# Two attentions in one program: when the second one starts, and what GpSimd does beside VectorE's trees

## The chip, the cores and the metric

One core of a Trainium2 chip. The metric is the device time of one execution in microseconds (us). A kernel is run several times and the median is given; one further execution is taken by the hardware profiler, and all readings of the trace are of that one. The span is the time from the first to the last instruction of the program on the core.

## The reference

Two multi-head layers over 2048 tokens of width 512, with 32 heads of 16, each with its own input and weights. A is softmax attention; B is linear attention with a feature map of two softmaxes. The result is both outputs side by side.

```
def A(x, wqkv, wo):
    q, k, v = heads(x @ wqkv)                          # 32 heads, 2048 x 16 each
    p = softmax(q @ k.T * 16 ** -0.5)                  # 2048 x 2048 for each head
    return concat_heads(p @ v) @ wo

def B(x, wqkv, w_phi, wo):
    q, k, v = heads(x @ wqkv)
    pq, pk = q @ w_phi, k @ w_phi                      # 16 x 16 for each head
    phi_q = [softmax(pq), softmax(-pq)]                # 32 features
    phi_k = [softmax(pk), softmax(-pk)]
    kv, z = phi_k.T @ v, phi_k.sum(tokens)
    return concat_heads((phi_q @ kv) / (phi_q @ z + 1e-6)) @ wo

out = concatenate([A, B], axis=-1)                     # 2048 x 1024, bfloat16
```

## The kernel before, in words

The program is written by a planner. A Python loop at the end of the function walks through numbered steps and appends instructions to one list for each engine (`_Plan`); each operation names what it depends on, and the plan turns that into semaphore waits. The loop chooses what TensorE does next by a small model of the engines' clocks (`_Clock`): the numbers in it decide only the order of the instructions. On the chip each engine takes its list strictly in order, and an instruction that waits holds up all that stands behind it on its engine. SyncE's list holds nearly all DMAs, in order as well.

**Attention A.** Heads are taken four at a time (a group g, rows 32r of the PE array for the four), queries 512 at a time (c): 8 x 4 = 32 units. A unit is cut into segments of 128-query tiles (`SPLIT`: mostly 2 and 2, the first unit 1, 1, 2, the last 2, 1, 1). Each of the 1024 steps (`order`) takes one query tile, one chunk of 512 keys (kc) and one pair of heads:

- `emit_m1` (L974): two matmuls put the scores of 128 queries x 512 keys for two heads into two PSUM banks; four banks are used by turns.
- `emit_r1` (L988): VectorE takes the maximum over the keys, 128 x 1024 values in one reduction.
- When a segment's steps are done, `emit_mchain` joins the maxima of the key chunks (L998, VectorE), GpSimd splits the negated maximum into two bfloat16 parts (L1004 to L1007), SyncE transposes them (L1009) and writes them as extra rows into QT (L1011). With them the scores come out with the maximum subtracted.
- From `LAGX` = 8 steps after the segment's end on, `block_go` computes the scores again, transposed, 512 columns in a block (L1041), ScalarE takes the exponential (L1048) into one of `RING` = 15 buffers, and `pv_go` multiplies with V (L1094). A column of ones in V gives the sum. There are 2048 blocks.
- After a unit, `emit_xev` copies the sums and products out (X, L458), `emit_rec` takes the reciprocals (a power on GpSimd, L1214) and spreads them by DMA (L1216, L1219), and `emit_mul` divides (L1229, GpSimd). `oproj_job` and, for the last 512 queries, `acc_job` and `emit_last` apply the output matrix (L1298 writes the last of it).

Where TensorE would have little to do, the planner puts in matmuls of zeros (L1178, L1193), which change nothing in the result.

**The head.** x comes in four chunks of 512 tokens by transposing DMAs on SyncE (L302). The weights for K and Q of the first groups come on ScalarE's queue, V's weights (columns 1024 to 1536) on SyncE's queue behind the third chunk of x (`load_w`, L296). `proj` computes K, Q and V (L498, L485); a chunk of keys can be scored only when its K exists. The table `XA` tells the planner from which time on it may order work on a chunk of x. The steps of the first segment need a new chunk of keys every two steps; two steps of the second segment are put in behind the first two.

**Attention B** fills gaps. 32 feature maps (`fm`, 16 for K, then 16 for Q) are planned from step `FM0` on, one every `FMSTEP` steps. Of a map: four matmuls and a copy by ScalarE (pB); two maps together go through `red`, a tree of eight small maxima and minima on VectorE (L660, L663, L665); then on GpSimd the subtraction (`sub`, L680, L682), on ScalarE the exponential (`ex`, L688), on GpSimd `sums` (L695 to L706), for K maps `rec` (a power, L718), and `mul` (L738). Four K maps at a time are multiplied with V (`kv_job`, added up by L794, masked by L798). A Q map goes on through a transposing DMA (`q_t`, L815), a matmul (`y_job`, L823), a copy to yB by ScalarE, `q_rc` (L841, L843 and a power, L846) and `q_mul` (L853) on GpSimd, a second transposing DMA (L862) into oTB, the output matmul (`ob_job`, L870), a copy to outB by ScalarE and the DMA to the output (L877). One Q map's `y_job` may only be planned when the `q_mul` of the map before it is. `pool_slot` hands out GpSimd's time in steps, so that planned work doesn't meet; `later(step, f)` runs f when the planner comes to a step; `add_job` queues matmuls for a gap from a step on, due at `by`.

Of the kernel before, what the change touches and what calls it, by code (L numbers as in the profile page):

```python
# [49 lines left out]
class _Plan:  # L50

    def __init__(self):
        self.streams = {}

    def add_stream(self, key, sem, step=1):
        self.streams[key] = _Stream(key, sem, step)

    def op(self, key, fn, deps=(), signal=True):
        s = self.streams[key]
        need = s.merge(deps)  # L60
        if not signal:
            s.items.append((fn, need, None))
            return None
        s.seq += 1
        clock = dict(s.known)
        clock[key] = s.seq
        s.items.append((fn, need, key))
        return _Tok(key, s.seq, clock)
# [80 lines left out]
def bass_concat_heads__softmax_full_mha__linear_kernel_hedgehog__prompt_kernel(  # L149
# [12 lines left out]
    SPLIT = {**{u: (2, 2) for u in range(NU)}, 0: (1, 1, 2), NU - 1: (2, 1, 1)}  # L162
    RING = 15
    BATCH = 4
    PIECE = 1
# [11 lines left out]
    TOP = 12.0  # L177
    FM0 = 172
    FMSTEP = 26
    units = [(g, c) for c in range(NQC) for g in range(NG)]  # L180
# [10 lines left out]
    for v, (u, q0, nq) in enumerate(segs):  # L191
        steps = [(v, pr, qt, kc) for kc in range(NKC) for qt in range(q0, q0 + nq) for pr in range(2)]
        if u == 0 and v == 1:
            order[2:2] = steps[0:2]
            steps = steps[2:]
        order += steps
# [9 lines left out]
    with contextlib.ExitStack() as es:  # L206
# [87 lines left out]

        def load_w(queue, lo, hi):
            t_wa[lo] = P.dma(queue, dsem("wa%d" % lo), lambda e: e.dma_start(wA[:, :, lo:hi], wa_v[:, :, lo:hi]))  # L296

# [3 lines left out]
        for c in range(NQC):  # L301
            t_xa[c] = P.dma("sp", dsem("xa%d" % c), lambda e, c=c: e.dma_start_transpose(  # L302
                xAT[:, :, c * 512:(c + 1) * 512], A_x[0][c * 512:(c + 1) * 512, :]))
            if c == 2:
                load_w("sp", 1024, 1536)
        load_w("sp", 128, 512)
# [51 lines left out]
        def later(slot, fn):  # L358
            calls.setdefault(slot, []).append(fn)

        pool_busy = [(q - 1, q + 2) for q in seg_end]

# [17 lines left out]

        ck = _Clock(8.5)
        ring_free = [(0.0, 4), (0.0, 5), (0.0, 6)]
# [153 lines left out]

        XA = (6.0, 11.0, 14.5, 18.5)
        need = [(4, "k", 0, 1), (6, "k", 0, 2), (8, "k", 0, 3)]
        need += [(LAG + 2 + kt, "v", kt, 0) for kt in range(NKT)]
        need += [(32 + 8 * c, "k", 1, c) for c in range(NKC)] + [(31, "q", 1, 0)]  # L540
        for at, t in enumerate(sorted(need)):
            c = t[2] // 4 if t[1] == "v" else t[3]
            add_job(at, *proj(*t[1:]), by=t[0] - 4, when=lambda c=c: ck.pe > XA[c])
        at = 30
        for g in range(2, NG, 2):
            for t in group(g):
                add_job(at, *proj(*t), by=at + 10)
                at += 6
        at = 200
        for c in range(1, NQC):  # L550
# [7 lines left out]
        for b, kind in ((4, "k"), (5, "q")):  # L558
# [3 lines left out]
            bank_reader[b] = fin(b, tok, 0)  # L562
        ck.act = 9.0

# [59 lines left out]
        for i in range(8):  # L624
            add_job(146 + 3 * i, *fold_job(1 - i // 4, i % 4), by=150 + 3 * i)

        kv_last = {}

        def fm(n):
# [8 lines left out]
            def p_fin(b, tok, tau):  # L638
                cx["p"] = aevac(pB[:, i, :], PS[:, b, :], [tok] + use(("p", i)))
                later(tau + 2, lambda: red(tau + 2))  # L640
                return cx["p"]
# [11 lines left out]
            def red(tau):  # L653
# [8 lines left out]
                for w in (4, 2):  # L662
# [5 lines left out]
                    [ts[k]] + use(("m", 0)) + use(("m", 1))) for k in range(2)]  # L668
                ck.extra += 1.85
                for c in (cx, first_map[0]):  # L670
                    c["mx"] = c["mn"] = ts[1]
                s = pool_slot(tau + 3, 2)
                later(s, lambda fn=first_map[1]: fn(s))
# [54 lines left out]
            def mul(tau):  # L728
# [15 lines left out]
                if x == 1:  # L744
                    kst[st] = cx
                    if st % 4 == 3:
                        for hf in range(2):
                            add_job(tau + 4, *kv_job(st // 4, hf))
                else:
                    later(tau + 4, lambda: q_t(st, cx, tau + 4))  # L750
# [61 lines left out]
        def q_t(st, cx, tau):  # L812
            i = st % 2
            k = st % 4
            cx["pt"] = P.dma("sp", d_pt[i], lambda e: e.dma_start_transpose(phiT[:, i], phiB[k]),  # L815
                             [cx["phi"], last_proj["q"]] + use(("pt", i)))
            users[("phi", k)] = [cx["pt"]]
            for hf in range(2):
                add_job(tau + 10, *y_job(st, cx, hf), when=lambda: st == 0 or st - 1 in q_done)

# [30 lines left out]
        def q_mul(st, cx, tau):  # L851
# [9 lines left out]
            def tr():  # L861
                cx["ot"] = P.dma("sp", d_ot[i], lambda e: e.dma_start_transpose(oTB[:, i], oB),  # L862
                                 [t] + use(("ot", i)))
                users[("o", 0)] = [cx["ot"]]
                add_job(tau + 14, *ob_job(st, cx))
            later(tau + 3, tr)
# [14 lines left out]

        first_map = []
        for n in range(2 * NKT):
            fm(n)
# [137 lines left out]
        def block_go(tau):  # L1022
# [11 lines left out]
            ck.run_tiled(r, start)  # L1034
            ck.heat.append((start, 0.25))
            g, c = units[u]
            slot = B % RING
# [37 lines left out]
        def pv_go(tau):  # L1075
# [15 lines left out]
            for j in range(per):  # L1091
                for B in Bs:
# [7 lines left out]
                    deps = []  # L1100
            ck.run_full("col", start, ck.ROW + 0.01)
            ck.heat.append((start, 1.0))
# [333 lines left out]
```

## Time and profile before

| | us |
|---|---|
| median of 3 runs | 1305.03 (1292.47 to 1312.32) |
| the profiled execution | 1295.11 |
| its span | 1293.4 |
| PE busy | 1222.3 (95%) |
| VectorE (DVE) busy | 1213.8 (94%) |
| ScalarE (ACT) busy | 1165.0 (90%) |
| GpSimd (POOL) busy | 632.8 (49%) |
| mean granted TensorE clock | 0.984 |

How to read it: busy time is the union of an engine's instructions; waits on semaphores and the issuing of DMAs are not counted. Reductions of VectorE overlap a little at their ends, so that their mean of 1215 ns is longer than the distance from one to the next. A row of a timeline gives the start, the time to the end of the last of the merged instructions, the engine, the line, what is written and read, and in brackets the idle time of the engine ahead of it and who ended it. SPq is SyncE's queue: its time is that of issuing, not of the transfer. The granted clock is the share of TensorE's full clock that the throttle let through.

### The profile page before, as it was taken

The numbers are of one execution on the slowest core, as the hardware profiler recorded it, in microseconds if no ns is written. First come the engines' busy times: TensorE is split into PE (matmuls) and PEld (weight loads), VectorE is DVE, ScalarE is ACT, GpSimd is POOL, SyncE is SP. The second block draws the span as 40 slices with busy tenths as digits, with TensorE's granted clock in tenths as the row PEclk, the third lists the DMA queues.
The fourth block names the chain that finished last, engine by engine and source line by source line (L and its number), as shares of the span: only waits on it lengthen the run. The fifth ranks groups of instructions, "written<-read, shape, count | busy, mean of one in ns | idle before, by whom it ended". The sixth has DMA issues, their size and how long they took to land.

```text
span 1293.4 us, 38893 instructions
## 1 busy us (share of the span) xinstructions
PE 1222.3 (95%) x16990; PEld 487.5 (38%) x16990; DVE 1213.8 (94%) x1229; ACT 1165.0 (90%) x2296; POOL 632.8 (49%) x724
## 2 busy tenths in 40 slices
PE   7999999999999999999999999999999999999998
PEld 2433333333333333334333333333333333333346
DVE  6999999999999899999999999999999999999930
ACT  3899999998988899999999989999989999999993
POOL 3311020255556465566574654565555466556562
PEclk9999999999999799999999989999989999999999
DMA  6134200001011001101101002121211121123121
GB/s 132 37 60 78 41 9 9 8 8 13 9 15 20 7 11 11 12 8 13 12 9 17 15 8 25 17 32 17 33 12 30 27 33 18 31 23 29 13 34 40
DMA packets 84259, 31.55 MB, mean 24 GB/s; under 512 B 71864, under 2 KB 82104, under 8 KB 84088
## 3 DMA queue, kind: packets, MB, share of 16 engines
q1 hardware_dynamic: 82744, 28.54, 15.8%
q8 instruction: 133, 2.18, 0.7%
q10 hardware_dynamic: 1344, 0.52, 0.2%
q14 instruction: 38, 0.31, 0.1%
HBM read 3.16 MB, written 4.19 MB: 6 GB/s over the span
## 4 chain that ended last, share of the span: by engine, by line
ACT 51%; PE 29%; DVE 18%; issue 1%; DMA 1%; SPq 1%; POOL 0%; DVEq 0%; ACTq 0%
ACT pT L1048 45%; DVE part L988 16%; PE PS L1041 6%; PE PS L974 4%; PE PS L1193 4%; PE PS L1094 3%; PE PS L1178 2%; PE PS L498 2%; PE PS L643 2%; ACT eB L688 1%; PE PS L485 1%; PE PS L870 1%; PE PS L898 1%; ACT X L458 1%; ACT pB L458 1%
## 5 line engine op out<-in xcount | busy, mean ns | idle before, releaser
L988 DVE TENSOR_REDUCE part<-PS 128x2 f32<-128x1024 f32 x1024 | 1174.8, 1215 | 21.6 <-PE PS L974 9.9
L1048 ACT ACTIVATE pT<-PS 128x512 bf16<-128x512 f32 x2048 | 1055.2, 636 | 75.4 <-PE PS L1041 38.1
L1041 PE MATMUL PS<-QT,KT 32*128 32x256 bf16 (+1 forms) x4224 | 666.1, 272 | 19.6 <-ACT pT L1048 2.1
L1178 PE MATMUL PS<-zmv,ones_t 32*128 32x512 bf16 x1755 | 595.9, 387 | 0.6 <-ACT X L458 0.4
L974 PE MATMUL PS<-KT,QT 32*128 32x512 bf16 x2048 | 452.1, 388 | 17.3 <-DVE part L988 11.8
L1041 PEld LDWEIGHTS PS<-QT,KT 32*128 32x128 bf16 x4224 | 226.5, 92 | 369.7 <-ACT pT L1048 222.9
L1004 POOL TENSOR_SCALAR stage<-mrow 128x8 bf16<-128x8 f32 (+1 forms) x66 | 15.8, 239 | 466.6 <-DVE mrow L998 466.6
L1094 PE MATMUL PS<-pT,VP 128*17 128x256 bf16 (+1 forms) x4224 | 205.5, 275 | 14.0 <-ACT pT L1048 4.8
L1193 PE MATMUL PS<-zmv,ones_t 128*17 128x256 bf16 x3640 | 169.0, 279 | 2.5 <-ACT X L458 2.0
L974 PEld LDWEIGHTS PS<-KT,QT 32*128 32x128 bf16 x2048 | 118.4, 91 | 110.3 <-DVE part L988 74.8
L1178 PEld LDWEIGHTS PS<-zmv,ones_t 32*128 32x128 bf16 x1755 | 144.2, 91 | 3.0 <-PE PS L1178 1.2
L1094 PEld LDWEIGHTS PS<-pT,VP 128*17 128x17 bf16 x4224 | 62.3, 88 | 125.1 <-ACT pT L1048 60.2
L1193 PEld LDWEIGHTS PS<-zmv,ones_t 128*17 128x17 bf16 x3640 | 73.5, 90 | 88.6 <-issue 77.7
L1214 POOL TENSOR_TENSOR lr<-lr,neg 128x16 f32<-128x16 f32 x31 | 90.6, 2922 | 16.9 <-DMA lr<-X 16.9
L846 POOL TENSOR_TENSOR den_t<-den_t,neg 128x32 f32<-128x32 f32 x16 | 87.5, 5467 | 1.3
L718 POOL TENSOR_TENSOR wB<-wB,neg 128x32 f32<-128x32 f32 x16 | 87.0, 5440 | 0.1
L1229 POOL TENSOR_TENSOR QT<-X,Yd 128x256 bf16<-128x256 f32 x62 | 44.0, 731 | 66.8 <-DMA Yd<-Yd 66.8
L738 POOL TENSOR_TENSOR wA<-eB,rB 128x512 bf16<-128x512 bf16 x64 | 66.9, 1069 | 0.6
L680 POOL TENSOR_TENSOR uB<-pB,mB 128x512 f32<-128x512 bf16 x32 | 33.5, 1047 | 27.4 <-DVE mB L665 27.4
L695 POOL TENSOR_TENSOR sB<-eB 128x512 f32<-128x512 bf16 x32 | 36.9, 1153 | 11.8 <-ACT eB L688 11.8
L643 PE MATMUL PS<-WKp,xBT 128*128 128x512 bf16 x128 | 38.0, 389 | 1.8 <-ACT pT L1048 0.2
L698 POOL TENSOR_TENSOR sB<-sB 128x256 f32<-128x256 f32 x64 | 36.1, 564 | 5.0
(90 smaller groups left out, 586.2 us busy)
## 6 DMA issues: line engine op xcount, KB each, us to landing
Yd<-Yd SPq DMA_DIRECT2D x124, 32.0 KB, 3.2
out_dram<-xAT SPq DMA_DIRECT2D x16, 128.0 KB, 1.9
KT<-oct_t SPq DMA_DIRECT2D x24, 64.0 KB, 2.1
QT<-oct_t SPq DMA_DIRECT2D x24, 64.0 KB, 2.0
out_dram<-OA SPq DMA_DIRECT2D x12, 128.0 KB, 1.8
mcols<-stage SPq DMA_TRANSPOSE x66, 2.2
QT<-mcols SPq DMA_DIRECT2D x62, 4.0 KB
wA<-in_A_wqkv_dram SPq DMA_DIRECT2D x2, 384.0 KB, 4.9
```

The costliest lines, as they stand in the source:

```text
L643: add_job(slot, mm_pieces(lambda e, b, ct: e.matmul(PS[:, b, :], xBT[:, ct, st * 128:(st + 1) * 128], Wf[:, x, ct, :], start=(ct == 0), st ...
L718: t = P.op("pool", lambda e: e.tensor_tensor(wB[:, n % 4, :], wB[:, n % 4, :], neg1[:, 0:1].broadcast_to([128, 32]), ALU.pow), [cx["r"], t ...
L738: t = P.op("pool", lambda e, a=a: e.tensor_tensor(f4[:, :, a, :], e4[:, :, a, :], r2[:, :, 1 - a].unsqueeze(2).broadcast_to([128, H, 16]), ...
L846: cx["rd"] = P.op("pool", lambda e: e.tensor_tensor(den_t[:, :], den_t[:, :], neg1[:, 0:1].broadcast_to([128, 32]), ALU.pow), [t, t_neg])
L974: tok = P.op("pe", lambda e, r=r, bank=2 * (q1 % 2) + i: e.matmul(PS[:, bank, :], QT[32 * r:32 * r + 32, g, q0:q0 + 128], KT[32 * r:32 * r ...
L988: r1[q1] = P.op("dve", lambda e: e.tensor_reduce(part[:, u % 2, 2 * pr:2 * pr + 2, qt, kc], PS[:, b:b + 2, :], AX.X, ALU.max), deps)
L1041: m2_t[B] = P.op("pe", lambda e, j=j: e.matmul(PS[:, bank, j * w:j * w + w], KT[32 * r:32 * r + 32, g, (kt + j) * 128:(kt + j + 1) * 128], ...
L1048: exp_t[B] = P.op("act", lambda e: e.activation(pT[:, slot, :], PS[:, bank, :], ACT.Exp, scale=0.25), [m2_t[B], slot_reader.get(slot)])
L1094: tok = P.op("pe", lambda e, B=B, r=r, j=j: e.matmul(PVB[32 * r:32 * r + 17, lo:lo + w], VP[:, kt + j, 4 * g + r, :], pT[:, B % RING, j * ...
L1178: fill_tok[0] = P.op("pe", lambda e: e.matmul(PS[:, 7, :], ones_t[32 * r:32 * r + 32, :], zmv[32 * r:32 * r + 32, :], start=False, stop=Fa ...
L1193: P.op("pe", lambda e, cq=cq: e.matmul(PS[32 * cq:32 * cq + 17, bank, 0:256], ones_t[:, 0:17], zmv[:, 0:256], start=(bank != 7), stop=(ban ...
L1214: rec = P.op("pool", lambda e: e.tensor_tensor(lr[:, ub, :], lr[:, ub, :], neg1[:, 0:1].broadcast_to([128, 16]), ALU.pow), [lr_t[u], t_neg])
```

## The change

- B's feature maps are planned from step 152 instead of 172 (`FM0`), one every 25 steps instead of 26 (`FMSTEP`); the folding of B's weights (`fold_job`) and A's later Q projections are planned 20 to 30 steps sooner. `y_job` is planned 8 instead of 10 steps behind the first transpose, `ob_job` 9 instead of 14 behind `q_mul`. `kv_job` may only be planned when the V parts of its four maps are.
- `_Plan.fence`: behind each tree, the first operation that the plan appends to GpSimd's list also waits for the tree's last operation. `red` is put in a slot in which GpSimd has nothing planned; the slots reserved at a segment's end are shortened by one step at the front.
- V's weights are loaded on ScalarE's queue when the first chunk of x has landed, no longer on SyncE's.
- Six steps of the second segment stand among those of the first instead of two: two behind each of its first three pairs (`EARLY`). The first segment ends at step 14 instead of 10, so the first exponentials are planned from step 22 instead of 18.
- Constants of the planner's clock model change: its start, `XA`, and a small charge for blocks that are made of several matmuls.

The built programs hold the same number of operations on VectorE (1229) and GpSimd (720); one DMA moves from SyncE's list to ScalarE's, and TensorE's list has 16274 matmuls instead of 16990, the difference being matmuls of zeros.

```
@@ class _Plan
+        self.fence = []
...
     def op(self, key, fn, deps=(), signal=True):
         s = self.streams[key]
+        if key == "pool" and self.fence:
+            deps = list(deps) + self.fence
+            del self.fence[:]
         need = s.merge(deps)
...
+    EARLY = 3
-    FM0 = 172
-    FMSTEP = 26
+    FM0 = 152
+    FMSTEP = 25
...
         if u == 0 and v == 1:
-            order[2:2] = steps[0:2]
-            steps = steps[2:]
+            for k in range(EARLY):
+                order[2 + 4 * k:2 + 4 * k] = steps[2 * k:2 * k + 2]
+            steps = steps[2 * EARLY:]
...
-        def load_w(queue, lo, hi):
-            t_wa[lo] = P.dma(queue, dsem("wa%d" % lo), lambda e: e.dma_start(wA[:, :, lo:hi], wa_v[:, :, lo:hi]))
+        def load_w(queue, lo, hi, deps=()):
+            t_wa[lo] = P.dma(queue, dsem("wa%d" % lo), lambda e: e.dma_start(wA[:, :, lo:hi], wa_v[:, :, lo:hi]), deps)
...
-            if c == 2:
-                load_w("sp", 1024, 1536)
+            if c == 0:
+                load_w("act", 1024, 1536, [t_xa[0]])
...
-        pool_busy = [(q - 1, q + 2) for q in seg_end]
+        pool_busy = [(q, q + 2) for q in seg_end]
...
-        ck = _Clock(8.5)
+        ck = _Clock(9.6)
...
-        XA = (6.0, 11.0, 14.5, 18.5)
+        XA = (6.0, 11.2, 14.0, 18.6)
...
-            add_job(at, *proj(*t[1:]), by=t[0] - 4, when=lambda c=c: ck.pe > XA[c])
+            add_job(at, *proj(*t[1:]), by=t[0] - 4, when=lambda c=c, v=t[1] == "v": ck.pe > max(XA[c], 11.8 * v))
...
-        at = 200
+        at = 170
...
-        ck.act = 9.0
+        ck.act = 9.6
...
-            add_job(146 + 3 * i, *fold_job(1 - i // 4, i % 4), by=150 + 3 * i)
+            add_job(125 + 3 * i, *fold_job(1 - i // 4, i % 4), by=130 + 3 * i)
...
@@ def p_fin
-                later(tau + 2, lambda: red(tau + 2))
+                s = tau + 2 if i == 0 else pool_slot(tau + 2, 3) + 1
+                later(s, lambda: red(s))
@@ def red
+                fence.append(ts[1])
...
-                s = pool_slot(tau + 3, 2)
+                s = pool_slot(tau + 2, 2)
@@ def mul
-                            add_job(tau + 4, *kv_job(st // 4, hf))
+                            add_job(tau + 4, *kv_job(st // 4, hf), when=lambda: all(
+                                "v" in kst.get(4 * (st // 4) + j, ()) for j in range(4)))
@@ def q_t
-                add_job(tau + 10, *y_job(st, cx, hf), when=lambda: st == 0 or st - 1 in q_done)
+                add_job(tau + 8, *y_job(st, cx, hf), when=lambda: st == 0 or st - 1 in q_done)
@@ def q_mul
-                add_job(tau + 14, *ob_job(st, cx))
+                add_job(tau + 9, *ob_job(st, cx))
...
+        P.fence = fence = []
...
@@ def block_go
+            start += 0.012 * (per - 1)
+            ck.rows[r] += 0.012 * (per - 1)
@@ def pv_go
-            ck.run_full("col", start, ck.ROW + 0.01)
+            ck.run_full("col", start, ck.ROW + 0.01 + 0.008 * (per - 1))
```

## The prediction, made before the changed kernel ran

> **What bounds the kernel now.** I read the busy shares and the costliest groups first, then the timelines of the two ends of the span, and last the stretches in which the granted clock fell.
>
> ```profile
> DVE  6999999999999899999999999999999999999930
> ACT  3899999998988899999999989999989999999993
> ...
> PEclk9999999999999799999999989999989999999999
> ...
> L988 DVE TENSOR_REDUCE part<-PS 128x2 f32<-128x1024 f32 x1024 | 1174.8, 1215 | 21.6 <-PE PS L974 9.9
> ```
>
> VectorE's 1024 maximum reductions (one a step, emit_r1) set the pace: they follow each other every 1.13 us, 1024 x 1.13 = 1157 us of a span of 1293.4 us. The first starts at 10.19 us, the last ends at 1239.6 us, so a step takes 1.20 us in the mean; then 53.8 us follow without reductions. The time above 1157 us lies in four places: that end, the head, the trees and the clock.
>
> The end, timeline of ScalarE and then of SyncE from 1240 us on:
>
> ```profile
> 1268.11 0.60 ACT L458 ACTIVATE xAT<-PS 128x512 bf16<-128x512 f32 x1 [1.13 <-PE PS L870]
> ...
> 1277.64 0.60 ACT L458 ACTIVATE xAT<-PS 128x512 bf16<-128x512 f32 x1 [5.12 <-PE PS L870]
> 1289.22 0.60 ACT L458 ACTIVATE xAT<-PS 128x512 bf16<-128x512 f32 x1 [10.98 <-PE PS L870]
> ```
>
> ```profile
> 1271.19 1.69 SPq L1298 DMA_DIRECT2D out_dram<-eB x2
> ...
> 1278.65 1.19 SPq L862 DMA_TRANSPOSE xAT<-WQp  x1
> 1289.84 0.34 SPq L877 DMA_DIRECT2D out_dram<-xAT  x1
> ```
>
> A's last output (L1298) is issued at 1272.54 and lands some 3.2 us later (fastest landing of that line), at 1275.7. All behind it is B: two more results through L862 and L870, with ScalarE idle 5.12 and 10.98 us between them. B's last output (L877) lands 1.7 us after 1289.84, at 1291.5.
>
> A tree (the pairwise maxima and minima of L660 to L665) by itself and beside GpSimd, VectorE's timeline, then GpSimd's:
>
> ```profile
> 245.44 0.75 DVE L660 TENSOR_TENSOR uB<-pB 128x512 bf16<-128x512 bf16 x2
> ...
> 247.24 3.52 DVE L988 TENSOR_REDUCE part<-PS 128x2 f32<-128x1024 f32 x3
> ```
>
> ```profile
> 370.03 1.73 DVE L660 TENSOR_TENSOR uB<-pB 128x512 bf16<-128x512 bf16 x2
> ...
> 372.82 2.34 DVE L988 TENSOR_REDUCE part<-PS 128x2 f32<-128x1024 f32 x2
> ```
>
> ```profile
> 369.88 1.60 POOL L1229 TENSOR_TENSOR QT<-X,Yd 128x256 bf16<-128x256 f32 x2
> ```
>
> Alone, a tree holds up the reductions for 247.24 - 245.44 = 1.80 us; beside two products of L1229 for 2.79 us. The same reading gives 3.28 us at 429.81 (beside L738 and L1214), 2.89 at 501.05 (L1229) and 2.84 at 747.84 (L794, L798): 0.99 + 1.48 + 1.09 + 1.04 = 4.6 us for four of the sixteen trees.
>
> The stretches in which TensorE had half its clock, as a table (span, then busy time of PE, PEld, DVE, ACT, POOL, granted clock):
>
> ```profile
> 433.00:454.50 21.50, 20.19 (x198) 6.16 (x197) 16.16 (x16) 15.49 (x29) 8.24 (x10) 0.52 0.12 8
> 754.80:765.10 10.30, 10.30 (x111) 3.50 (x110) 7.77 (x9) 7.72 (x15) 5.08 (x9) 0.50 0.02 5
> 846.90:850.50 3.60, 3.50 (x47) 1.08 (x46) 2.41 (x3) 2.92 (x7) 2.58 (x1) 0.53 0.02 5
> 963.00:970.00 7.00, 7.00 (x65) 2.08 (x66) 4.41 (x4) 4.51 (x8) 2.42 (x5) 0.51 0.46 38
> ```
>
> In them VectorE idles 5.34 + 2.53 + 1.19 + 2.59 = 11.7 us. The first two begin 4 and 7 us after the crowded trees at 429.81 and 747.84; the fourth follows a wait of ScalarE for GpSimd's L853 (2.9 us at 959.8).
>
> The head, VectorE's timeline:
>
> ```profile
> 10.19 3.49 DVE L988 TENSOR_REDUCE part<-PS 128x2 f32<-128x1024 f32 x3 [0.49 <-PE PS L974]
> 14.56 1.23 DVE L988 TENSOR_REDUCE part<-PS 128x2 f32<-128x1024 f32 x1 [0.89 <-PE PS L974]
> 16.27 2.36 DVE L988 TENSOR_REDUCE part<-PS 128x2 f32<-128x1024 f32 x2 [0.48 <-PE PS L974]
> 19.28 2.36 DVE L988 TENSOR_REDUCE part<-PS 128x2 f32<-128x1024 f32 x2 [0.65 <-PE PS L974]
> 23.15 3.49 DVE L988 TENSOR_REDUCE part<-PS 128x2 f32<-128x1024 f32 x3 [1.51 <-PE PS L974]
> ```
>
> Behind the first start, four waits of 0.89 + 0.48 + 0.65 + 1.51 = 3.5 us for the next chunk of K.
>
> **The change part by part**, against the profiled execution, 1295.1 us (span 1293.4).
>
> B sooner and closer (FM0, FMSTEP). The last map's planned step goes from 172 + 31 x 26 = 978 to 152 + 31 x 25 = 927: 51 steps, 51 x 1.20 = 61 us. B's last output then lands near 1230 us, well before A's. The chain from last map to last output keeps its length, some 105 us (evictions of pB at 1186 us, landing at 1291.5); even 30 us more would stay covered. The span now ends with A: 1275.7 against 1291.5 is -15.8 us. Of B's work inside A's own last 36 us, ScalarE loses four L458 evictions of yB (1.5 us), two of outB (1.2 us) and 1.1 us of waiting for L870: 3.8 us at most, nothing if 45 exponentials wait for something else; I take -2.5. The same work now lies in the middle, beside reductions. There ScalarE was busy 930 of the 1000 us from 200 to 1200; a map costs it 0.60 + 1.08 + about 0.6 us, 2.3 us, and at 25 steps instead of 26 this is 0.3% of its time more. I take 0, at most +3 (0.3% of 1000 us, if all of it became backlog).
>
> Trees on an idle GpSimd (Plan.fence, and red now asks for a free slot). At most -4.6, at least 0; ten of the sixteen fences fall on L680, which needed the tree anyway, so they add nothing; the other six hold an L1229, an L794, a power or the start of q_rc for at most one tree, 1.8 us. Queued behind them is B's work, with slack since B is off the end, and once a maximum split (L1004), whose blocks are due eight steps (9.6 us) later and whose row was sent off 3.2 us (median) to 7.4 us after the maximum here. I take -4. A sentence of the Trainium skill, "SBUF — State Buffer", "SBUF: two separate sides", calls VectorE's and GpSimd's shared port an exclusive lock held for the whole instruction. By it a tree that meets a power would wait for all of its 2.9 or 5.5 us, and as four fences have a power right ahead of them in GpSimd's queue, up to 4 x 2.9 = 11.6 us would be given back, 1276. This trace agrees for products, not for powers: the tree at 820.55 ran beside the 5.55 us of L846 and took 1.95 us.
>
> Clock. If the crowded trees opened the two stretches behind them, 5.34 + 2.53 = 7.9 us go with them. The bounds are -11.7 (no fall at all) and 0 (others fall instead). I take -5.
>
> Head (EARLY = 3, V's weights). Six steps of the second part now stand between the chunks of K, two behind each pair, so each chunk has 4 x 1.13 = 4.5 us instead of 2.3; K's second chunk also stands ahead of the first V projection, which waited at 12.73 us for V's weights. At most -3.5, at least 0; I take -3, as the chunks' projections took about 3 us from pair to pair in the rows above. V's weights (512 KB) leave SyncE's queue: the fourth transpose of x and all behind it are issued 0.6 us sooner. On ScalarE's queue they wait for x's first chunk (6.45 us); nothing stands behind them there before the first eviction at 13.8 us. The first part now ends at step 14 instead of 10 and the exponentials begin four steps later in number, 4.5 us, of which 3 us are made up: +1 at worst, taken as 0. A sentence of the Trainium skill, "Trainium Kernel Development and Optimization", "Key Constraints", speaks against this part: queues share the same 16 DMA engines, so a second one saves issue time alone. The engines' share is 0.70 from 10 to 26 us, at 142 GB/s; by it 512 KB among x's chunks could take 3.6 us from them and the head's term would be 0, 1268.
>
> Waits of B on transposes (y_job 2 steps sooner, ob_job 5 steps or 6 us sooner). In the last stage above, L862's result lands 4.1 us (its slowest) after 1278.65 and L870 starts at 1288.15: 5.4 us later. With 6 us less TensorE would stop 0.6 us; the other stages have more, so 0. kv_job's new condition holds a job until its V exists: 0.
>
> Sum: -15.8 - 2.5 - 4 - 5 - 3 = -30.3, 1264.8 us. The profiled execution is 9.9 us under the median of the runs shown (1305.03; 1292.47 to 1312.32). Nothing in VectorE's durations can make such a spread (1202 to 1229 ns each), so I put it to the clock stretches, which the change thins out, and add nothing to the value but 10 us to the upper bound.
>
> **Rivals.** (1) Only the end is gained: the planner writes a new order on every engine, other trees or waits open as many clock stretches, the head waits for V's weights. 1295.1 - 15.8 - 2.5 = 1277, up to 1287 with the median's 10 us. For it: the stretch at 846.9 follows no tree. Against: crowding is what the fence forbids. (2) The clock falls nowhere and all bounds are met: 1295.1 - 15.8 - 3.8 - 4.6 - 11.7 - 3.5 = 1256. (3) Slower: the transposes of B come late. TensorE takes its matmuls in order; with 5 steps less, an L862 that GpSimd releases one power (5.5 us) late makes L870 wait about 5 us, with all scores and blocks behind it, and a stretch of half clock follows (2.9 us in the mean of four): 8 us each. Sixteen of them cost 128 us, 1393; from eight on (64 us against 30 gained) it is slower by over 2%. For it: B's q chain is serial, and GpSimd was late at 959.8. Against: the margin of the last stage was 5.4 us even there.
>
> **Numbers.** Forecast 0.66, (1) 0.20, (2) 0.09, (3) 0.05. Faster or slower by 2%, about what a measurement of this kernel tells from no change, lies at 1279 and 1331. Faster: nine tenths of the forecast, three tenths of rival (1) and all of (2), 0.74. Slower: rival (3) and a remainder of 0.01, 0.06. Within 2%: 0.20. Range 1250 to 1288: from rival (2) with the landings a little shorter to the upper end of (1).
>
> **What would show it.** After the last reduction, no L870 or L862 work and the last landing A's own (36 us or less behind it); every tree within 1.8 to 2.0 us and GpSimd silent beside it; no VectorE wait over 0.3 us in the first 30 us; fewer or shorter stretches of half clock, above all none just behind a tree. It is wrong if B's output still ends last, if trees of 2.8 us remain, if TensorE waits for a DMA of L815 or L862, or if half-clock time stays above 40 us.

## The result, and the profile after

The changed kernel takes 1286.74 us (median of 20 runs, 1273.2 to 1297.6), the kernel before 1297.2 us in the runs made beside it (20 runs, 1291.78 to 1315.18). The ratio is 0.9904 with a 95% interval of 0.9878 to 0.9931: about 1% faster, not the 2.5% of the forecast, and within the 2% either way that the prediction counted as no change and gave a chance of 0.20. The time lies inside the range and 21.9 us above the forecast of 1264.8.

The profiled execution of the changed kernel took 1293.89 us and is one of its longest, with a mean granted clock of 0.960 where its runs have 0.969 at the median; the stretches of half clock below are therefore somewhat longer than usual. In the changed kernel the line numbers of everything used here are higher: emit_r1 is L998, the block L1053, its exponential L1060, `y_job` L832, `q_mul` L862, the second transpose L871, `ob_job` L879, B's output L886, A's last output L1310.

The page of the changed kernel, VectorE, ScalarE and the granted clock in 40 slices, and the group of the reductions (busy us, mean ns | idle time ahead of them and what ended most of it):

```profile
DVE  7999999999999999999999999999997998799860
ACT  3899999999999999998998999999996898799777
PEclk9999999999999999999999999999996998799759
...
L998 DVE TENSOR_REDUCE part<-PS 128x2 f32<-128x1024 f32 x1024 | 1175.9, 1216 | 43.1 <-PE PS L1190 15.8
```

A reduction takes what it took before (1216 ns against 1215), but the idle time ahead of the 1024 has doubled, 43.1 us against 21.6. Of it 34 us lie in slices 31, 34, 35, 38 and 39, exactly where the clock row shows 6, 8, 7, 7 and 5. Of the rest 4.5 us lie in slices 25 and 26, where the clock fell twice for 3.41 us, and 1.8 us in the first slice.

The end, SyncE's timeline from 1278 us on, and then VectorE's last rows:

```profile
1288.45 1.69 SPq L1310 DMA_DIRECT2D out_dram<-eB  x2
```

```profile
1254.39 2.36 DVE L998 TENSOR_REDUCE part<-PS 128x2 f32<-128x1024 f32 x2 [0.93 <-PE PS L984]
1256.78 0.17 DVE L1008 TENSOR_REDUCE mrow<-part 128x4 f32<-128x16 f32 x1
```

A's own output is the last; no L871 and no L886 stands behind it. From the last maximum to the end of the span it is 35.4 us instead of 53.8.

A tree, VectorE's timeline and then GpSimd's beside it:

```profile
223.75 0.75 DVE L667 TENSOR_TENSOR uB<-pB 128x512 bf16<-128x512 bf16 x2
...
225.54 1.23 DVE L998 TENSOR_REDUCE part<-PS 128x2 f32<-128x1024 f32 x1
```

```profile
225.72 1.05 POOL L688 TENSOR_TENSOR uB<-pB,mB 128x512 f32<-128x512 bf16 x1 [10.02 <-DVE mB L672]
```

225.54 - 223.75 = 1.79 us, with GpSimd silent until the tree is over. All sixteen are like that.

The head, VectorE's timeline:

```profile
9.75 3.49 DVE L998 TENSOR_REDUCE part<-PS 128x2 f32<-128x1024 f32 x3 [0.49 <-PE PS L984]
13.87 1.23 DVE L998 TENSOR_REDUCE part<-PS 128x2 f32<-128x1024 f32 x1 [0.63 <-PE PS L984]
15.59 12.89 DVE L998 TENSOR_REDUCE part<-PS 128x2 f32<-128x1024 f32 x11 [0.50 <-PE PS L984]
```

Behind the first start VectorE waits 0.63 + 0.50 = 1.1 us where it waited 3.5. In this execution the clock was at half for 3.41 us from 11.8 us on.

So three of the four parts of the forecast are there. What has been added is in TensorE's waits (released by, total us, times, longest):

```profile
PE PS L879 <- DMA xAT<-WQp: 12.3, 7, 2.8
PE PS L984 <- DVE part L998: 9.2, 27, 1.3
```

The first row has no counterpart in the profile before: seven times `ob_job`'s matmul stood at the head of TensorE's list waiting for the second transpose, L871. Three of the seven, in TensorE's timeline:

```profile
969.11 1.46 PE L879 MATMUL PS<-woB,xAT 128*128 128x512 bf16 x3 [2.82 <-DMA xAT<-WQp]
...
1195.79 0.39 PE L879 MATMUL PS<-woB,xAT 128*128 128x512 bf16 x1 [2.30 <-DMA xAT<-WQp]
...
1216.32 0.71 PE L879 MATMUL PS<-woB,xAT 128*128 128x512 bf16 x2 [1.48 <-DMA xAT<-WQp]
```

And the same places as a table by stretches (span, then busy time of PE, PEld, DVE, ACT, POOL, granted clock, DMA share, GB/s):

```profile
964.00:967.50 3.50, 2.28 (x35) 0.90 (x34) 3.50 (x4) 3.31 (x7) 3.37 (x1) 1.00 0.71 44
967.50:991.40 23.90, 22.30 (x170) 6.46 (x170) 14.88 (x14) 13.62 (x25) 12.23 (x20) 0.50 0.06 13
...
1216.70:1254.20 37.50, 37.50 (x355) 12.22 (x354) 26.80 (x24) 26.28 (x49) 5.35 (x10) 0.50 0.12 17
```

In the 3.50 us in which the longest wait (2.82 us) began TensorE worked 2.28 us; then the clock was 0.50 for 23.9 us, in which VectorE worked 14.88 us and so idled 9.0. The last wait, of 1.48 us, was followed by 37.5 us of half clock and 10.7 us of idle VectorE. Each of the seven waits has such a fall within 2 us of it: 3.41 us at 790.0, 3.41 at 810.5, 23.89 at 967.5, 10.24 at 1073.3, 17.07 at 1104.1, 3.41 at 1196.2 and 37.55 at 1216.7, together 99 us. The profile before had 41 us in four stretches. At the median clock of 0.969 half-clock time would be some 80 us, an estimate (2 x 0.031 x 1285).

Why the transpose came late is in SyncE's timeline around the first of these waits, behind GpSimd's row of `q_mul`:

```profile
951.61 1.06 POOL L862 TENSOR_TENSOR WQp<-WQp,den_t 128x512 bf16<-128x512 f32 x1
```

```profile
949.21 0.62 SPq L1221 DMA_DIRECT2D lr<-X  x1
958.25 1.14 SPq L1019 DMA_TRANSPOSE mcols<-stage  x1
960.49 0.64 SPq L1021 DMA_DIRECT2D QT<-mcols  x1
961.17 0.57 SPq L1228 DMA_DIRECT2D Yd<-lr  x1
963.00 2.47 SPq L1231 DMA_DIRECT2D Yd<-Yd  x4
965.52 1.26 SPq L871 DMA_TRANSPOSE xAT<-WQp  x1
```

The data of L871 were ready at 952.67. It was issued at 965.52, 12.9 us later, because SyncE's list is taken in order and the maxima's transpose, its write into QT and the spreading of the reciprocals stood ahead of it, each waiting for its own producer. It took 3.5 us to land, at 969.06, and L879 started at 969.11. Over the sixteen stages of B this delay on SyncE was 0 to 8.8 us before (mean 2.7) and is 0 to 14.9 us now (mean 7.2).

### The profile page after: what moved, and what is told of

The parts are those of the page before. It is cut to its first block, busy times and chain, and to the rows that moved or that the text cites. A ratio compares the mean times of both kernels' runs of the same rounds, so it can differ in the third digit from the quotient of the medians.

```text
span 1292.2 us, 37487 instructions
## 1 busy us (share of the span) xinstructions
PE 1221.7 (95%) x16274; PEld 474.5 (37%) x16274; DVE 1210.0 (94%) x1229; ACT 1166.4 (90%) x2296; POOL 630.9 (49%) x724
## 4 chain that ended last, share of the span: by engine, by line
ACT 38%; DVE 27%; PE 26%; DMA 4%; POOL 3%; SPq 1%; issue 1%; ACTq 0%; POOLq 0%
ACT pT L1060 34%; DVE part L998 25%; PE PS L1053 7%; PE PS L984 4%; PE PS L1106 3%; PE PS L504 2%; PE PS L1190 2%; PE PS L1205 2%; DMA xAT<-WQp 2%; PE PS L650 1%; ACT eB L696 1%; PE PS L491 1%; PE PS L879 1%; DMA mcols<-stage 1%; PE PS L908 1%
## 5 line engine op out<-in xcount | busy, mean ns | idle before, releaser
L998 DVE TENSOR_REDUCE part<-PS 128x2 f32<-128x1024 f32 x1024 | 1175.9, 1216 | 43.1 <-PE PS L1190 15.8
L1060 ACT ACTIVATE pT<-PS 128x512 bf16<-128x512 f32 x2048 | 1063.1, 641 | 96.3 <-PE PS L1053 44.5
L1053 PE MATMUL PS<-QT,KT 32*128 32x256 bf16 (+1 forms) x4224 | 681.3, 276 | 17.4 <-ACT pT L1060 1.2
L984 PE MATMUL PS<-KT,QT 32*128 32x512 bf16 x2048 | 463.0, 396 | 13.4 <-DVE part L998 9.2
L1053 PEld LDWEIGHTS PS<-QT,KT 32*128 32x128 bf16 x4224 | 231.7, 93 | 374.0 <-ACT pT L1060 214.1
L1106 PE MATMUL PS<-pT,VP 128*17 128x256 bf16 (+1 forms) x4224 | 208.8, 278 | 11.5 <-ACT pT L1060 2.3
L1205 PE MATMUL PS<-zmv,ones_t 128*17 128x256 bf16 x2952 | 147.9, 283 | 1.2
L1205 PEld LDWEIGHTS PS<-zmv,ones_t 128*17 128x17 bf16 x2952 | 57.6, 90 | 81.2 <-issue 71.9
```

Of the source, the lines that this page charges most:

```text
L984: tok = P.op("pe", lambda e, r=r, bank=2 * (q1 % 2) + i: e.matmul(PS[:, bank, :], QT[32 * r:32 * r + 32, g, q0:q0 + 128], KT[32 * r:32 * r ...
L998: r1[q1] = P.op("dve", lambda e: e.tensor_reduce(part[:, u % 2, 2 * pr:2 * pr + 2, qt, kc], PS[:, b:b + 2, :], AX.X, ALU.max), deps)
L1053: m2_t[B] = P.op("pe", lambda e, j=j: e.matmul(PS[:, bank, j * w:j * w + w], KT[32 * r:32 * r + 32, g, (kt + j) * 128:(kt + j + 1) * 128], ...
L1060: exp_t[B] = P.op("act", lambda e: e.activation(pT[:, slot, :], PS[:, bank, :], ACT.Exp, scale=0.25), [m2_t[B], slot_reader.get(slot)])
L1106: tok = P.op("pe", lambda e, B=B, r=r, j=j: e.matmul(PVB[32 * r:32 * r + 17, lo:lo + w], VP[:, kt + j, 4 * g + r, :], pT[:, B % RING, j * ...
L1205: P.op("pe", lambda e, cq=cq: e.matmul(PS[32 * cq:32 * cq + 17, bank, 0:256], ones_t[:, 0:17], zmv[:, 0:256], start=(bank != 7), stop=(ban ...
```

## The experiments

Two theories. **T**: the loss is the waits of TensorE for the second transposes, which the plan puts 6 steps ahead of their matmuls (`tr` at +3, `ob_job` at +9) and which SyncE issues late, with the half clock that each wait sets off. **R**: the loss is not in these waits: the new order of work itself leaves TensorE thinner (716 fewer matmuls of zeros), so that the clock falls whatever the transposes do.

All ratios are against the kernel before on the same chip. As each run has its own mean granted clock, a straight line of time against it can be laid through the runs of a kernel: 1283.5 us + 769 x (1 - clock) for the kernel before (55 runs, correlation 0.98), 1261.6 + 815 x (1 - clock) for the changed one (17 runs, 0.96). "At full clock" below means the first term of such a line, and is an extrapolation.

**e1: the changed kernel with `ob_job` 14 steps behind `q_mul` again.**

```
-                add_job(tau + 9, *ob_job(st, cx))
+                add_job(tau + 14, *ob_job(st, cx))
```

> The changed kernel with one edit: ob_job is planned 14 steps behind q_mul again instead of 9. Theory T (late transposes): all seven stretches of half clock behind step 600 of the changed kernel began at a wait of TensorE's output matmul of B (L879) for the second transpose (L871). With 5 more steps (6 us) nearly all seven waits (1.1 to 2.8 us) go, half-clock time falls from 99 us to 40 us or less, and the time comes to 1262 to 1272 us (the sum of the prediction without its blind spot), a ratio to before near 0.975. Rival R (the new order): B ends at step 1000 and is packed closer, so TensorE has less in some windows and the clock falls there anyway, waits or not: half-clock time stays at 80 to 110 us and the time at 1283 to 1290.

1254.72 us (6 runs, 1252.02 to 1266.96), ratio 0.9699 (0.9664 to 0.9735). Its page's clock row, and the largest of its waits of TensorE:

```profile
PEclk9999999999999999999999999999999999999999
```

```profile
PE PS L984 <- DVE part L998: 12.6, 36, 1.3
PE PS L650 <- ACT pT L1060: 4.6, 15, 0.4
```

No wait for a transpose is left, and the clock falls once, for 3.41 us at 897.8, beside a wait of 0.93 us for a copy by ScalarE. At full clock the kernel takes 1251.1 us, 10.5 us less than the changed one, which is about the 12.3 us of waits. The rest of the 32 us between the medians (27 by the ratios) is the clock. The time is lower than the 1262 to 1272 that T gave. This fits T; but the order of all else moved a little too, so R is not excluded by it.

**e2: the kernel before with `ob_job` at 9 steps.**

```
-                add_job(tau + 14, *ob_job(st, cx))
+                add_job(tau + 9, *ob_job(st, cx))
```

> The kernel before with one part of the change alone: ob_job 9 steps behind q_mul instead of 14. T: waits of TensorE for the second transpose appear (at least three of 16, as the margins of before, 5 to 14 us, shrink by 6 us and SyncE's queue is as full), each followed by half clock; half-clock time rises from about 41 us to 60 or more, and although the last output is planned some 5 us sooner, the time is no better than before: 1297 to 1310. R: the waits alone do nothing to the clock; the shorter end gives 1290 to 1294.

1309.88 us (12 runs, 1298.34 to 1321.83), ratio 1.0081 (1.0046 to 1.0115). The trace has one wait of the output matmul, 1.6 us at 985.6, without a fall, and not the three or more that T expected. Half clock is 51 us, in other places (20.48 us at 438.0, 17.07 at 758.8). The edit costs 0.8%, all of it by the clock (1283.1 us at full clock), but T's mechanism is not what it shows: five steps alone do not make the waits. The delay of the second transposes on SyncE is 4.1 us in the mean here against 7.2 in the changed kernel; which other part of the change adds the rest, no run isolates. The two long falls stand beside waits of TensorE for VectorE (1.31 us and 1.25 us), at trees that ran beside GpSimd and took 3.28 and 2.83 us, as in the kernel before; 3.41 us at 943.1 lie beside a wait of 0.92 us for a first transpose.

**e3: the changed kernel with more matmuls of zeros.**

```
-    COLD = 7.0
-    WARM = 7.4
+    COLD = 8.0
+    WARM = 8.4
```

> The changed kernel with ob_job left at 9 steps, but the planner told to keep TensorE busier with matmuls of zeros (COLD 8.0 instead of 7.0, WARM 8.4 instead of 7.4). R: the thin windows are filled, half clock falls below 40 us and the time to 1272 or less. T: matmuls of zeros stand behind the waiting matmul like everything else, so the waits for L871 stay (five or more) and each still opens a stretch; these may end sooner as the windows behind them hold more work: 1275 to 1290.

1276.89 us (4 runs, 1274.81 to 1278.08), ratio 0.985 (0.9827 to 0.9874). The clock is full (0.9985), but with 18582 matmuls in TensorE's list instead of 16274, the difference being zeros, ScalarE falls behind: 89 exponentials come after the last maximum, 47 in e1. The new plan happened to have one wait for a second transpose (1.35 us) instead of seven. The time lies in the range that T gave, but not for T's reason. So the clock is held up both by more work and by fewer waits, and the run does not tell T from R.

**e4: e1 with B planned at its former times.**

```
-    FM0 = 152
-    FMSTEP = 25
+    FM0 = 173
+    FMSTEP = 26
```

> The changed kernel with ob_job at 14 steps, and B planned from step 173, one map every 26 steps (the last map at step 979, as before; step 172 itself is not used). It keeps the fence, the head and the rest. By the prediction's terms it loses the end: +15.8 +2.5 = 18 us on the kernel with ob_job at 14 alone, so 1282 to 1290 if T is right, with B's output landing 12 us or more behind A's. If R is right and the packing is what costs the clock, half-clock time is that of before (about 40 us) here and the time is at or below that of the kernel with ob_job at 14 and B early.

1289.63 us (12 runs, 1275.95 to 1311.26), ratio 0.9905 (0.9872 to 0.9937): 35 us above e1, 20 to 21 us at full clock. SyncE's timeline at its end:

```profile
1259.01 1.69 SPq L1310 DMA_DIRECT2D out_dram<-eB  x2
...
1264.49 2.16 SPq L871 DMA_TRANSPOSE xAT<-WQp  x1
1274.47 0.33 SPq L886 DMA_DIRECT2D out_dram<-xAT  x1
```

B is last again: its output lands at 1276.1 us, 12 us behind A's (1264.0). B's earlier start is the largest gain of the change.

**e5: e1 without the fence and without the free slot for the trees.**

```
-                s = tau + 2 if i == 0 else pool_slot(tau + 2, 3) + 1
+                s = tau + 2
...
-                fence.append(ts[1])
```

> The kernel with ob_job at 14 steps, without the fence and without the free slot for the trees. By the prediction's terms trees run beside GpSimd again: up to 4.6 us longer over all 16, and a stretch of half clock behind one or two of them: 1258 to 1272 against 1254.7. If the fence itself costs (GpSimd held up), it is at or below 1254.

1263.8 us (6 runs, 1257.31 to 1268.77), ratio 0.9737 (0.9696 to 0.9777). 9.1 us above e1 by the medians, 5 us by the ratios (0.38% of 1297), 4.2 us at full clock; the intervals of the two overlap, so the sign is likely and the size is not settled. Three of its trees run beside GpSimd again and take 2.29, 2.67 and 3.74 us, together 3.3 us more than three of 1.80. Behind the longest TensorE waits 1.02 us for VectorE, and 10.24 us of half clock follow at 1016.3. The trace has a new wait of its own besides, 3.8 us for a first transpose at 742.4, with 6.83 us of half clock beside it.

**e6: e1 with the head as before.**

```
-    EARLY = 3
+    EARLY = 1
...
-            if c == 0:
-                load_w("act", 1024, 1536, [t_xa[0]])
+            if c == 2:
+                load_w("sp", 1024, 1536)
...
-        XA = (6.0, 11.2, 14.0, 18.6)
+        XA = (6.0, 12.1, 15.6, 19.6)
```

> The kernel with ob_job at 14 steps and the head as before: EARLY 1, V's weights on SyncE's queue behind the third chunk of x, XA moved to the old times. By the prediction's term of 3 us (0 to 3.5): 1256 to 1259 against 1254.7, VectorE waiting 3 to 4 us in the first 27 us. If V's weights on the second queue slow down x's chunks, no difference or the reverse.

1262.41 us (6 runs, 1260.19 to 1264.59), ratio 0.9724 (0.9693 to 0.9755): 7.7 us above e1 by the medians, more than expected, 3 by the ratios (overlapping intervals again), 5.4 at full clock. VectorE's timeline in the head of e6, then of e1:

```profile
15.30 2.36 DVE L998 TENSOR_REDUCE part<-PS 128x2 f32<-128x1024 f32 x2 [0.58 <-PE PS L984]
20.34 2.36 DVE L998 TENSOR_REDUCE part<-PS 128x2 f32<-128x1024 f32 x2 [2.68 <-PE PS L984]
26.20 3.49 DVE L998 TENSOR_REDUCE part<-PS 128x2 f32<-128x1024 f32 x3 [3.51 <-PE PS L984]
```

```profile
9.73 17.20 DVE L998 TENSOR_REDUCE part<-PS 128x2 f32<-128x1024 f32 x15 [0.49 <-PE PS L984]
```

0.58 + 2.68 + 3.51 = 6.8 us of waits against none in fifteen reductions. Part of the 6.8 is a fall of the clock at 14.06 us for 10.2 us in this execution. V's weights on ScalarE's queue do hold up x: its third chunk lands at 12.28 us in e1 and at 10.47 here, but no reduction of e1 waits for it.

**e7: e1 with `y_job` at 10 steps again.**

```
-                add_job(tau + 8, *y_job(st, cx, hf), when=...)
+                add_job(tau + 10, *y_job(st, cx, hf), when=...)
```

> The kernel with ob_job at 14 steps and y_job at 10 steps again, so both of B's waits on transposes as before the change. T: the first transpose (L824) was not late (its margins were 0.2 us and more), so 1252 to 1258, no difference to 1254.7 beyond 0.3%.

1252.9 us (6 runs, 1251.73 to 1256.58), ratio 0.9654 (0.9623 to 0.9685), the fastest of all: 3.5% under the kernel before. Against e1 it is within the intervals; the spread of its runs is small, 4.9 us against 14.9.

**e8: the changed kernel with the second transpose put into SyncE's list at once.** `ob_job` stays at +9.

```
-            later(tau + 3, tr)
+            tr()
```

> The changed kernel with ob_job left at 9 steps, and the second transpose (tr) appended to SyncE's list at once behind q_mul instead of three steps later. The order of TensorE, VectorE, ScalarE and GpSimd is instruction for instruction that of the changed kernel; only the 16 transposes stand further ahead in SyncE's list. T: the transposes no longer stand behind the maxima's transposes and the spreading of the reciprocals (5 to 15 us of waiting each in the changed kernel), so at most two of the seven waits of L879 stay, half-clock time falls from 99 to 35 us or less, and the time to 1256 to 1268. R (the order and the packing): the same order gives the same thin windows, half clock stays at 80 to 110 us, 1283 to 1290.

The lists of TensorE, VectorE, ScalarE and GpSimd are the same as the changed kernel's, instruction for instruction, the matmuls of zeros included; only the place of L871 in SyncE's list differs. 1259.31 us (6 runs, 1258.44 to 1263.65), ratio 0.9706 (0.9675 to 0.9738). SyncE's timeline at the place shown above, and TensorE's `ob_job` there:

```profile
952.73 0.62 SPq L1221 DMA_DIRECT2D lr<-X  x1
956.23 1.22 SPq L871 DMA_TRANSPOSE xAT<-WQp  x1
961.78 1.12 SPq L1019 DMA_TRANSPOSE mcols<-stage  x1
```

```profile
970.00 0.81 PE L879 MATMUL PS<-woB,xAT 128*128 128x512 bf16 x3 [0.19 <-ACT pT L1060]
```

L871 is issued ahead of the maxima's transpose, has landed long before 970, and L879 no longer waits for it, here or anywhere. Over the sixteen stages the delay on SyncE is 1.1 us in the mean where it was 7.2, and half clock is 20.5 us where it was 99. 27 of the 32 us are back (26 of 27 by the ratios) with nothing moved but a DMA's place in a queue. By R nothing should have changed, so R falls as the main cause. What is left is a wait for the other transpose:

```profile
PE PS L984 <- DVE part L998: 9.5, 28, 1.3
PE PS L832 <- DMA WQp<-wA: 3.1, 1, 3.1
```

It ends at 820.77 and has 13.65 us of half clock from 818.3 on beside it.

**e9: e7 and e8 together** (`y_job` at 10, `ob_job` at 14, `tr()` at once).

```
-            later(tau + 3, tr)
+            tr()
```

> A version that could beat all others: ob_job at 14 steps, y_job at 10, and the second transpose appended to SyncE's list at once (order on the other four engines is that of the kernel with 14 and 10 steps). T: waits on both transposes gone already, so nothing more to gain but rare stretches of half clock: 1250 to 1256. If the earlier transposes hold up the maxima's transposes behind them on SyncE, blocks come late: 1255 to 1262.

1258.0 us (6 runs, 1253.92 to 1260.15), ratio 0.9711 (0.9682 to 0.9739): no gain over e7, rather 5 us lost. An early L871 now holds up what it passed: a block (L1053) waits 1.94 us at 1170.6 for the maxima's row that SyncE writes (L1021, issued at 1168.72, in e7 at 1166.00), and 3.41 us of half clock lie beside it. That is in a profiled execution of 1253.92 us, so the trace does not show all of the 5 us.

**e10: the changed kernel with `ob_job` at 12.**

```
-                add_job(tau + 9, *ob_job(st, cx))
+                add_job(tau + 12, *ob_job(st, cx))
```

> The changed kernel with ob_job at 12 steps behind q_mul, between the changed kernel's 9 and the 14 of before. T: a dose: 3 steps (3.6 us) cover waits of up to 2.8 us, so at most two waits of L879 stay, half-clock time is 15 to 40 us and the time 1255 to 1268, between 1254.7 (14 steps) and 1286.7 (9 steps) and nearer the former.

1258.51 us (6 runs, 1250.58 to 1270.05), ratio 0.9739 (0.9694 to 0.9783), without a wait for a transpose in the profiled execution, which took 1250.58 us. Three steps are enough there; what made the clock fall in longer runs of this kernel (to 0.977 in the longest) is not in the trace.

**e11: the changed kernel with `y_job` at 10 and `tr()` at once** (`ob_job` at 9).

```
-                add_job(tau + 8, *y_job(st, cx, hf), when=...)
+                add_job(tau + 10, *y_job(st, cx, hf), when=...)
...
-            later(tau + 3, tr)
+            tr()
```

> The changed kernel with the second transpose appended at once and y_job at 10 steps, ob_job left at 9. In the version with the early transpose and y_job at 8, one wait of 3.1 us for the first transpose (L824) stood before 13.7 us of half clock. T: with it gone the time is 1252 to 1258. R: no better than that version's 1259.3.

1257.79 us (6 runs, 1248.43 to 1265.96), ratio 0.9709 (0.9661 to 0.9758). The wait for a first transpose did not go (1.20 us at 819.83), and 40.96 us of half clock followed it in the profiled execution (1265.96 us), where the wait of 3.07 us in e8 has 13.65 beside it: the length of a stretch does not go by the length of the wait. The time lies at the upper end of the range that T gave, but not because the wait went.

**e12: e1 with the second transpose put into SyncE's list later.** The four engines' lists are e1's; L871 enters SyncE's list 8 steps behind `q_mul` instead of 3.

```
-            later(tau + 3, tr)
+            later(tau + 8, tr)
```

> The reverse: the kernel with ob_job at 14 steps (1254.7 us), whose second transpose is now appended to SyncE's list 8 steps behind q_mul instead of 3, so that 6 steps are left to the output matmul as in the changed kernel. The order on the other four engines is instruction for instruction that of the 1254.7 us kernel. T: the transposes stand behind the maxima's again, at least four waits of L879 of 1 us and more come back, half-clock time rises to 50 us or more and the time to 1270 to 1292. R: the order is that of the fast kernel, so is the time, 1252 to 1260.

1263.15 us (6 runs, 1260.34 to 1267.45), ratio 0.9757 (0.9725 to 0.9789). TensorE's largest waits, and one of the three in its timeline:

```profile
PE PS L984 <- DVE part L998: 9.3, 27, 1.3
PE PS L879 <- DMA xAT<-WQp: 8.1, 3, 4.2
```

```profile
970.46 1.03 PE L879 MATMUL PS<-woB,xAT 128*128 128x512 bf16 x2 [4.18 <-DMA xAT<-WQp]
```

The waits are back, with 6.83 us of half clock beside the first and 3.41 beside the third; the second (1.74 us) had none. The longest stretch, 17.07 us at 899.1, stands beside the wait of 0.93 us for ScalarE that e1 has too. It is 8.4 us slower than e1, so the sign is T's and R's 1252 to 1260 is missed, but three waits came instead of four or more, half clock is 31 us instead of 50 or more, and the price is 2 to 3 us each, under the range T gave. At full clock e12 takes 1258.1 us, 7.0 above e1: here the waits cost about their own length (8.1 us) and little through the clock. The intervals of e1 and e12 touch; that the waits cause the time rests on e8 first.

## Why the prediction was right or wrong

**The failed step is "Waits of B on transposes".** It took 5.4 us of margin between the landing of L862 (now L871) and the start of `ob_job` from the profile before, took 6 us off, and put the rest at 0 because "the other stages have more". In the profile before they did, 6.8 to 13.6 us. But that margin was not a property of the stage. It was what SyncE's queue left in the old order, and the same change that shortened the distance to 6 steps also moved L871 behind other waiting DMAs: the mean delay on SyncE went from 2.7 to 7.2 us, and in seven stages of sixteen the margin became 0. Two of the prediction's own signs of being wrong came true with it: TensorE waits for this DMA, and half-clock time is above 40 us. The prediction's own text says that TensorE takes its matmuls in order and that each such wait could bring a stretch of half clock; rival (3) had the mechanism, with GpSimd's power as the cause of lateness and 8 us a wait. The lateness was SyncE's queue, and the price about (10.5 + 18.4) / 7 = 4 us.

**Where the 21.9 us between forecast and result are**, by the lines through the runs: the waits 1261.6 - 1251.1 = +10.5; the clock, which costs 1286.7 - 1261.6 = 25.1 us at the median (clock 0.969) where the forecast had 6.7 left (11.7 - 5), +18.4; all other terms together -7.0 (e1 takes 1251.1 at full clock, the forecast without its 6.7 is 1258.1). So the other parts brought more than forecast, and the waits, with the clock put down to them, took back about 29 us.

**Clock.** The term of -5 had the wrong sign in the changed kernel: 99 us of half clock against 41. "None just behind a tree" came true for six of the seven falls, which came beside the new waits; the one at 1073.3 stands 1.9 us behind the tree of 1069.6 and 1.7 us behind a wait. Without the waits, in e1, half clock was 3.4 us, near the bound of -11.7. That the spread of the runs goes with the clock was right: both lines above have it, with correlations of 0.96 and 0.98, and the median of the kernel before (clock 0.983) follows from its line, 1283.5 + 769 x 0.017 = 1296.6.

How a crowded tree can come before a fall, the profile before shows in TensorE's timeline behind the trees of 429.81 and 747.84:

```profile
434.36 0.61 PE L974 MATMUL PS<-KT,QT 32*128 32x512 bf16 x2 [1.31 <-DVE part L988]
...
751.95 0.39 PE L974 MATMUL PS<-KT,QT 32*128 32x512 bf16 x2 [1.25 <-DVE part L988]
```

These are the longest waits of TensorE behind the head there, and the falls of 434.0 and 754.8 stand beside and 2.9 us behind them. The fence takes such waits away, and in e5, without it, one is back. So late trees and late transposes come to the same thing, a short wait of TensorE; that the waits of the trees cause their falls is not tested by itself.

**End.** Right: A's output last, 35.4 us behind the last maximum. Forecast -18.3, measured -20 to -21 at full clock (e4 against e1), and -35 with the clock that e4 loses.

**Trees.** Right in mechanism, all sixteen at 1.8 us and the fence at no visible cost. Forecast -4 and a clock term; e5, whose trees take 3.3 us more, gives -4.2 at full clock, and 5 to 9 us in all, with overlapping intervals.

**Head.** Forecast -3. The waits fell from 3.5 to 1.1 us, to none in e1, and e6 gives 3 to 7.7 us. By the rule of the Trainium skill that the prediction weighed ("Trainium Kernel Development and Optimization", "Key Constraints": queues share the DMA engines) the head's term would have been 0. The landings agree with the rule: with V's weights on ScalarE's queue the third chunk of x lands 1.8 us later (12.28 us in e1, 10.47 in e6). The term is not 0 all the same, because with the steps put in between no reduction of e1 waits for that chunk.

**Rivals.** (1), 1277 to 1287 with only the end gained, gives the measured time for another reason: trees and head were gained too. That the time lies inside the range is owed to the width this rival gave it, and so to luck. The bounds of (2), 1256, were met by e1 and passed by e7.

## What to carry to other kernels

The latency of a DMA includes the time it stands in an in-order issuing queue behind DMAs that wait for other producers; a margin read from one profile need not hold in another order, so when the distance between a DMA and its consumer is cut, follow the queue in the new order, not the old landing time. Waits of 1 to 3 us on a busy TensorE can cost more than twice their length through the clock (12.3 us of them cost about 29 us in the changed kernel, 8.1 us in e12 about 8), while the slack taken away here (five steps for one output matmul) gained nothing (e2: 1283.1 us at full clock against 1283.5). Before a part is judged by the total, undo one number at a time: here one constant hid two thirds of the gain (2.0 of 3.0% by the ratios).

## What the runs showed of the hardware that was not expected

The clock falls to 0.50 without TensorE having been idle for long: waits of 0.9 us were enough (e1 at 897.8, e2 at 943.1), and in the 3.5 us ahead of the fall at 967.5 it worked 2.28 us. It is not certain to fall (1.74 us in e12 and 1.6 us in e2 had no fall beside them). All falls of an execution start on one grid of 3.41 us. In the changed kernel TensorE was busy for 0.33 to 0.68 of the piece of this grid ahead of each of the seven falls; in every other piece at full clock between 14 and 1288 us it was busy for 0.77 or more. No sharp rule comes of it: a piece of e2 with 0.55 (1.87 us, up to 987.5) has no fall behind it, and the fall of e7 at 1137.4 follows a piece with 0.91 (3.11 us). A stretch lasts a multiple of 3.41 us, from 3.41 to 40.96, and one of 37.5 us went on although the trace shows TensorE busy in all of it. "TensorE: Matmul & The Clock Gate" of the Trainium skill, in "Part 1: The HAM clock gate", gives half rate after an idle window of about 3.4 us and full rate after a busy one. The step of 3.41 us agrees with these runs; the condition does not, in either direction, and the measurement decides.

Open: why a stretch once lasts 3.4 us and another time 41, what opens the stretches that have no wait of 0.8 us or more beside them (among others before at 847.0 and 963.1, e7 at 1137.4, e8 at 535.0 and 763.7), and which part of the change put the second transposes behind so much on SyncE. By the two lines a loss of 0.01 in the mean clock, which is about 26 us at half, costs 7.7 to 8.2 us: 0.3 us for each.
